# One order for the experts' stage on every engine, weights made in smaller steps, and first loads held back

## The chip, the cores and the metric

The kernel runs on one core of a Trainium2 chip. The core has five engines with a queue each: TensorE (PE; its weight loads are listed as PEld), VectorE (DVE), ScalarE (ACT), GpSimd (POOL) and SyncE (SP), which here issues all DMAs. An engine takes the instructions of its queue one after the other. The metric is the device time of one execution in microseconds; the median of several runs counts.

## What is computed

Attention with clusters, then a soft mixture of experts on its result. Sizes: 4 batches, 8 heads, 768 rows, 64 columns; 16 clusters; 8 experts with 512 x 1024 and 1024 x 512 weights, applied to all 3072 rows.

```python
q_assign = argmax(einsum('bhsd,hcd->bhsc', q_n, c_n))     # q_n, k_n, c_n: normalised rows
k_assign = argmax(einsum('bhsd,hcd->bhsc', k_n, c_n))
mask = q_assign[..., :, None] == k_assign[..., None, :]
attn = softmax(where(mask, scale * q @ k.T, -1e9))
x = (attn @ v) transposed to [3072, 512]
P = exp(x @ w_gate - max); 8 times: rows to sum 1, columns to sum 1, times N / E
out = sum over e of P[:, e:e+1] * (max(x @ w1[e], 0) @ w2[e])
```

## The kernel before

**Attention.** The class Planner (line 58) runs one generator ("process") for each piece of a head's work: load_pair (q and k of two heads), load_group (v of four heads, with their sums), split_part, assign_pair and place_pair (clusters, mask, and moves between tiles by DMA), max_chunk and max_rows (row maxima), exp_chunk, values, norm, out_batch (stores x of a batch to HBM as xd[b], and the gate logits lg), first_x (splits the first batch's x for the experts) and scan_first (largest weights of expert 0, 8 times two loads into a tile with one buffer, each followed by a reduce on VectorE). A process yields an engine with an assumed cost, or an event or token to wait for; the planner's own clock and the keys in KEYS decide who issues next. After every step keep_order ties each new instruction to the one before it on its engine, so the queues hold attention's work in just the planned order. The planner orders; it does not wait on the chip.

**Experts' stage.** x and w1 are split in 16-bit high and low parts, and layer 1 of two blocks of 128 hidden columns is one step of Winograd's form of Strassen's scheme: seven products instead of eight. The loop over order takes (batch, expert) in the order (0,0), (1,0), (0,1), (1,1), ... for batches 0 and 1, then the same for 2 and 3. Each has NP2 = 4 blocks f2, so there are 128 iterations t, four for each of 32 pairs. An iteration runs layer1: seven products m = 0 to 6 (product, L1173; six matmuls each), which are evicted by add (DVE, L1195) or scaled (ACT, L1200); relu_split makes hh (ACT, L1184) and the remainder hl (DVE, L1185). Between the products the loop calls step(before): layer2 of the iteration before, six blocks of rows of six matmuls (L1235 to L1237), accumulated in PSUM over the four f2 and, after the last, weighted by the gate into acc (done, L1253 and L1255). PSUM holds two tiles h_ps for the products and everything else small (ps_h, h_tile), and six for layer 2.

Beside this the loop steps through other generators, some pieces per iteration, by the number m of the product just issued:
- making: make_w makes one set of weights (wa, wb) of a pair of blocks from raw tiles r1, r2 (two buffers, wp0 and wp1): a scaling of r1 (ACT, L1083), four sums (GpSimd, L1093), casts on ScalarE with a remainder on GpSimd for three groups (L1096 and L1097; L1104 and L1105; for wb L1101 and L1102), and a scaling of r2 (L1099). begin(idx) says in which iteration set idx is started; load_raw loads the next set's raw tiles (L1070, L1074) then. For batch 0 each set is stored to HBM (store_w, L1110, L1111); the other batches load it from there (load_w, L1116, L1117). Made sets have three buffers.
- scanning: scan finds the largest weights of a later expert, eight loads of 512 KB in two tiles (L279, L283), each followed by a reduce (DVE, L286), and then the scale through two small matmuls (powers, L238 and L248); scan_at says in which iteration it starts.
- inputs: next_x loads the next batch's four parts xq (L1149), takes their largest (L286), makes four differences (less, L296) and splits seven parts into high and low (L300 on ACT, L303 on DVE).
- sink: gates, the exponential and eight rounds of normalisation of the gates (L1021 to L1048).

In this stage nothing calls keep_order. The framework's scheduler places each instruction by its own estimate of times, within the data dependencies, and so may move work of this stage in front of other work on an engine, into attention's end too. Tiles of pools opened after attention lie where attention's pools (nat first) lay, and wait for their last readers there.

## Time and profile before

| | us |
|---|---|
| median of 3 runs | 2497.99 (2495.38 to 2498.4) |
| profiled execution, its own time | 2494.76 |
| its span, first to last instruction | 2492.9 |
| TensorE busy with matmuls | 2386.4 (96%) |
| VectorE / ScalarE / GpSimd busy | 1374.5 / 834.8 / 651.5 |
| mean granted share of TensorE's clock | 0.987 |

Times in the rows are counted from the span's start. A matmul's end is modelled, so TensorE shown as busy need not be at its peak: the distance of starts tells more. In a timeline a row is start, duration, engine (with q where it is the queue's own instruction, such as a DMA issue), line, operation, output<-inputs, shapes and count; brackets hold the engine's idle time before it and what ended it. The granted clock has two levels, 1.2 and 2.4 GHz; a share between them is a mean over a stretch.

### The profile page before, as it was taken

Reading aid. Unit: us, or ns where it says so; the run is one execution under the profiler, and the core shown is the slowest. Engines: PE = TensorE matmul, PEld = TensorE weight load, DVE = VectorE, ACT = ScalarE, POOL = GpSimd, SP = SyncE. Lnnn points to the kernel's source line nnn. Section 1 sums busy time; section 2 is a strip of 40 time slices with the busy share of each in tenths; the row PEclk is TensorE's granted clock in tenths of the full one; section 3 lists DMA queues with packets and bytes.
Section 4 is the critical chain, followed back from the end, with each engine's and each line's share of the span. In section 5 each row is a group of like instructions: output and inputs, shape, how many; then the busy total and the mean of one; then the engine's idle time right before and its main releaser. Section 6 shows DMA issues by size and latency. Waiting matters only on the chain.

```text
span 2492.9 us, 32750 instructions
## 1 busy us (share of the span) xinstructions
PE 2386.4 (96%) x12848; PEld 1275.2 (51%) x12848; DVE 1374.5 (55%) x2385; ACT 834.8 (33%) x1610; POOL 651.5 (26%) x697
## 2 busy tenths in 40 slices
PE   6999999987898999999999999999999999999999
PEld 3655555543444455555454555555555555555554
DVE  7888888859674544444444446544443444444443
ACT  3555555554333333333424222222121222212221
POOL 4776767753323323241414100000000000000000
PEclk8999999988999999999999999999999999999999
DMA  7555454337766442434333314332222223222322
GB/s 162 134 118 131 97 123 91 104 146 270 271 238 229 155 154 101 158 113 141 132 124 133 123 43 144 104 112 95 93 103 106 94 93 109 101 93 94 114 103 89
DMA packets 154683, 320.30 MB, mean 128 GB/s; under 512 B 61088, under 2 KB 90528, under 8 KB 154016
## 3 DMA queue, kind: packets, MB, share of 16 engines
q1 hardware_dynamic: 154528, 318.21, 40.0%
q8 instruction: 101, 1.65, 0.3%
q14 instruction: 54, 0.44, 0.1%
HBM read 230.74 MB, written 58.72 MB: 116 GB/s over the span
## 4 chain that ended last, share of the span: by engine, by line
PE 72%; POOL 8%; DVE 8%; DMA 6%; issue 4%; ACT 2%; SPq 0%; POOLq 0%; ACTq 0%; DVEq 0%
PE h_ps L1173 28%; PE o_ps L1235 10%; PE o_ps L1236 10%; PE o_ps L1237 10%; PE av_ps L817 3%; POOL r L1093 3%; DMA r<-in_moe_w 3%; PE max_ps L690 2%; PE exp_ps L758 2%; DMA scan<-in_moe_w 2%; DVE mrt L694 2%; PE exp_ps L759 2%; POOL wa L1105 2%; POOL wb L1102 2%; POOL wa L1097 1%
## 5 line engine op out<-in xcount | busy, mean ns | idle before, releaser
L1173 PEld LDWEIGHTS <-wa 128*128 128x128 f16 x5376 | 529.0, 98 | 474.7 <-issue 54.3
L1185 DVE SCALAR_TENSOR_TENSOR hl<-c,hh 128x384 f16<-128x384 f32 x512 | 312.5, 611 | 544.5 <-ACT hh L1184 544.3
L1173 PE MATMUL h_ps<-xsT,wa 128*128 128x384 f16 x3072 | 588.7, 328 | 12.8 <-DVE u L1195 6.7
L1237 PE MATMUL o_ps<-wb,hl 128*128 128x512 f16 x1536 | 583.6, 380 | 4.9 <-DVE hl L1185 4.9
L1235 PE MATMUL o_ps<-wb,hh 128*128 128x512 f16 x1536 | 584.2, 380 | 0.0
L1236 PE MATMUL o_ps<-wb,hh 128*128 128x512 f16 x1536 | 584.1, 380 | 0.0
L1184 ACT ACTIVATE hh<-c 128x384 f16<-128x384 f32 x512 | 266.9, 522 | 854.2 <-DVE c L1195 850.4
L1173 PE MATMUL h_ps<-xsB,wa 128*128 128x384 f16 x2304 | 425.6, 329 | 19.8 <-DVE c L1195 18.8
L1237 PEld LDWEIGHTS <-hl 128*128 128x128 f16 x1536 | 150.7, 98 | 186.7 <-DVE hl L1185 7.4
L1195 DVE SCALAR_TENSOR_TENSOR c<-h_ps,u 128x384 f32<-128x384 f32 x256 | 142.0, 555 | 181.7 <-PE h_ps L1173 180.0
L784 POOL TENSOR_TENSOR psum<-psum,pe 128x512 f32<-128x512 f32 (+1 forms) x198 | 215.9, 1107 | 51.4 <-ACT pe L765 46.2
L1195 DVE SCALAR_TENSOR_TENSOR u<-h_ps,m 128x384 f32<-128x384 f32 x256 | 141.8, 554 | 157.1 <-PE h_ps L1173 156.8
L1235 PEld LDWEIGHTS <-hh 128*128 128x128 f16 x1536 | 150.8, 98 | 140.4 <-issue 1.8
L1236 PEld LDWEIGHTS <-hh 128*128 128x128 f16 x1536 | 150.8, 98 | 139.6 <-issue 1.3
L694 DVE TENSOR_REDUCE mrt<-max_ps 128x1 f32<-128x512 f32 (+1 forms) x288 | 190.6, 682 | 32.0 <-PE max_ps L690 29.7
L1200 ACT ACTIVATE c<-h_ps 128x384 f32<-128x384 f32 x128 | 62.5, 489 | 412.3 <-PE h_ps L1173 412.2
L765 ACT ACTIVATE pe<-exp_ps 128x512 f32<-128x512 f32 x288 | 166.4, 596 | 90.9 <-PE exp_ps L759 82.5
L1097 POOL TENSOR_TENSOR wa<-r,wa 128x256 f16<-128x256 f32 (+1 forms) x62 | 59.7, 982 | 389.0 <-ACT wa L1096 389.0
L1255 DVE SCALAR_TENSOR_TENSOR acc<-o_ps,gates,acc 128x512 f32<-128x512 f32 x168 | 125.3, 746 | 45.0 <-PE o_ps L1237 45.0
L817 PE MATMUL av_ps<-pe,vn 128*64 128x512 f32 (+1 forms) x768 | 134.4, 492 | 0.0
L690 PE MATMUL max_ps<-kX,qX 96*128 96x256 f32 (+1 forms) x384 | 125.7, 388 | 7.2 <-DVE mrt L694 6.3
L1093 POOL TENSOR_TENSOR r<-r 128x256 f32<-128x256 f32 x124 | 97.5, 807 | 122.9 <-ACT r L1083 114.7
(195 smaller groups left out, 1988.1 us busy)
## 6 DMA issues: line engine op xcount, KB each, us to landing
wa<-wd SPq DMA_DIRECT2D x96, 896.0 KB
wb<-wd SPq DMA_DIRECT2D x96, 512.0 KB
r<-in_moe_w SPq DMA_DIRECT2D x64, 512.0 KB
wd<-wa SPq DMA_DIRECT2D x32, 896.0 KB
scan<-in_moe_w SPq DMA_DIRECT2D x56, 512.0 KB
wd<-wb SPq DMA_DIRECT2D x32, 512.0 KB
qn<-in_q SPq DMA_DIRECT2D x16, 384.0 KB
kn<-in_k SPq DMA_DIRECT2D x16, 384.0 KB
```

Source lines behind the costliest of these rows:

```text
L690: nc.tensor.matmul(ps[:, y * (z - a) : (y + 1) * (z - a)], t["qa"][0:96, i * P : (i + 1) * P], t["k2"][0:96, a:z], start=True, stop=True)
L694: nc.vector.tensor_reduce(out=t["mr"][:, i0 : i0 + ni, ni - 1], in_=ps.rearrange("p (x c) -> p x c", x=ni), axis=AX, op=ALU.max)
L784: (nc.gpsimd if e == POOL else nc.vector).tensor_tensor(out=st[:, a:z], in0=old[a], in1=part, op=ALU.add)
L817: nc.tensor.matmul(av[o, a:z], vn[:, i, :], heads[t]["pe", c][:, i - i0], start=(i == 0), stop=False, skip_group_check=True)
L1093: by.tensor_tensor(out=S_[:, o], in0=a, in1=b_, op=op)
L1173: nc.tensor.matmul(ps[:, 0:HB], wa[:, w_, a, c, :], x[:, x_, c, :], start=(first and s_ == 0), stop=(s_ == len(steps) - 1), skip_group_che ...
L1184: nc.scalar.activation(hh[:, 2 - i, o], src, AF.Relu)
L1185: nc.vector.scalar_tensor_tensor(out=hl[:, 2 - i, o], in0=src, scalar=0.0, in1=hh[:, 2 - i, o], op0=ALU.max, op1=ALU.subtract)
L1195: nc.vector.scalar_tensor_tensor(out=t, in0=ps[:, 0:HB], scalar=KAPPA, in1=x, op0=ALU.mult, op1=ALU.add)
L1235: nc.tensor.matmul(po[i], hh[:, t, ti], wbh[:, t], start=(first and t == 0), stop=False)
L1236: nc.tensor.matmul(po[i], hh[:, t, ti], wbl[:, t], start=False, stop=False)
L1237: nc.tensor.matmul(po[i], hl[:, t, ti], wbh[:, t], start=False, stop=(last and t == 1))
```

## The change

- Experts' stage: keep_order is called after each product of layer 1 with all that is stepped beside it, and at the end. So every engine's queue keeps the order of the trace, behind attention's last instruction on that engine.
- The remainder hl is kept back in a list (rests) and issued after the steps of sink, scanning and inputs, before layer 2's block and the weights.
- The steps go to other m: sink at 0, 3, 5; scanning at 0 and 3 (in iterations 7 to 10 also 2 and 5); inputs at 0, 2, 3, 5, 6. Before it was odd m for sink, m = 1 and 4 for scanning (in the first four iterations 1, 3, 4, 5), even m for inputs.
- make_w has five steps instead of six, in the order: scaling and sums; scaling of r2; the first casts; the casts of the sums; wb.
- The sets of expert 1 start in iterations 7, 8, 9, 10 instead of 4, 6, 8, 10, its neighbour's scan (expert 2) in 7 instead of 4; both scans have an iteration by which they are run to their end (6 and 10).
- next_x has two empty steps after its loads; its differences are computed on GpSimd, the first two earlier.
- Attention: load_pair from the third pair on waits until the maxima of head 0 are placed (ev rows 0), load_group of the second group until those of head 1 are; scan_first waits before each of its eight rounds for the values of heads 16 to 23. The v tiles get a pool of their own (vals).

```diff
@@ -291,9 +291,9 @@
     LESS = {"T2": (("T1", "B12", "B11"), ("T2", "B22", "T1")), "B21": (("T4", "B21", "T2"), ("T3", "B22", "B12"))}
     xq, xs = {}, [{} for _ in range(B)]
-    def less(o, a, c):
+    def less(o, a, c, by=nc.vector):
         t = tmp.tile([P, KC, HB], F32, name="tx")
-        nc.vector.tensor_tensor(out=t, in0=xq[a], in1=xq[c], op=ALU.subtract)
+        by.tensor_tensor(out=t, in0=xq[a], in1=xq[c], op=ALU.subtract)
         xq[o] = t
     def split_hi(b, o):
@@ -310,6 +310,7 @@
         brief = actx.enter_context(tc.tile_pool(name="brief", bufs=1))
         work = actx.enter_context(tc.tile_pool(name="work", bufs=2))
         sm = actx.enter_context(tc.tile_pool(name="sm", bufs=2))
+        vals = actx.enter_context(tc.tile_pool(name="vals", bufs=2))
         ps_m = actx.enter_context(tc.tile_pool(name="ps_m", bufs=2, space=PSUM))
         ps_s = actx.enter_context(tc.tile_pool(name="ps_s", bufs=2, space=PSUM))
         ps_x = actx.enter_context(tc.tile_pool(name="ps_x", bufs=2, space=PSUM))
@@ -468,7 +469,7 @@
         def load_pair(p):
             b, hp_ = divmod(p, NP)
-            if p > 1 and GATES[0]:
+            if p > 1:
                 yield ev["rows", 0]
             yield t_nat
             t = pairs[p] = {}
@@ -483,9 +484,11 @@
             b, g = n // H, n % H // G
             hs = slice(g * G, (g + 1) * G)
             yield t_vn
+            if n == G:
+                yield ev["rows", 1]
             t = groups[(b, g)] = {}
             yield SP, 0.625
-            vn = nat.tile([P, G, NT, D], F32, name="vn", bufs=2)
+            vn = vals.tile([P, G, NT, D], F32, name="vn")
             nc.sync.dma_start(
                 out=vn.rearrange("p h t d -> p h (t d)"), in_=v[b, hs].rearrange("h (p t) d -> p h (t d)", t=NT)
             )
@@ -954,6 +957,7 @@
         def scan_first():
             am8 = sm.tile([P, 2, NF], F32, name="am8", bufs=1)
             for f in range(NF):
+                yield ev["v", nheads // 2 + f]
                 for m in range(2):
                     yield SP, 0.625
                     t = sm.tile([P, 512], F32, name="scan0", bufs=1)
@@ -1081,7 +1085,6 @@
         wa, wb = wt
         raw = r1[:, 0 : 4 * KC * P]
         nc.scalar.activation(raw, raw, AF.Copy, scale=s1[:, e : e + 1])
-        yield
         A = raw.rearrange("p (k c t f) -> p t k c f", k=2, c=KC, t=2)
         S_ = r1[:, 4 * KC * P :].rearrange("p (o c f) -> p o c f", o=4, c=KC)
         for o, a, b_, op in (
@@ -1092,17 +1095,17 @@
         ):
             by.tensor_tensor(out=S_[:, o], in0=a, in1=b_, op=op)
         yield
+        nc.scalar.activation(r2, r2, AF.Copy, scale=s2[:, e : e + 1])
+        yield
         for o, a in ((A22, A[:, 0, 1]), (slice(A11, A12 + 1), A[:, 1])):
             nc.scalar.copy(wa[:, 0, o], a)
             by.tensor_tensor(out=wa[:, 1, o], in0=a, in1=wa[:, 0, o], op=ALU.subtract)
         yield
-        nc.scalar.activation(r2, r2, AF.Copy, scale=s2[:, e : e + 1])
+        nc.scalar.copy(wa[:, 0, 3:7], S_)
+        by.tensor_tensor(out=wa[:, 1, 3:7], in0=S_, in1=wa[:, 0, 3:7], op=ALU.subtract)
         yield
         nc.scalar.copy(wb[:, 0], r2)
         by.tensor_tensor(out=wb[:, 1], in0=r2, in1=wb[:, 0], op=ALU.subtract)
-        yield
-        nc.scalar.copy(wa[:, 0, 3:7], S_)
-        by.tensor_tensor(out=wa[:, 1, 3:7], in0=S_, in1=wa[:, 0, 3:7], op=ALU.subtract)
         yield
     def store_w(idx, wt):
@@ -1147,16 +1150,21 @@
             k, j = divmod(i, 2)
             xq[o] = pers.tile([P, KC, HB], F32, name=f"xq{o}", tag=xq_from[o][1])
             nc.sync.dma_start(out=xq[o], in_=xd[b][:, k * KC : (k + 1) * KC, j * HB : (j + 1) * HB])
+        yield
+        yield
         for i, o in enumerate(XQ):
             largest(am4[:, i : i + 1], xq[o].rearrange("p c s -> p (c s)"))
             yield
+        for t, a, c in LESS["T2"]:
+            less(t, a, c, nc.gpsimd)
         am = gs.tile([P, 1], F32, name="am")
         nc.vector.tensor_reduce(out=am, in_=am4, axis=AX, op=ALU.max)
         for _ in input_scale(b, am, h_tile, gs):
             yield
         for o in XS:
-            for t, a, c in LESS.get(o, ()):
-                less(t, a, c)
+            if o == "B21":
+                for t, a, c in LESS[o]:
+                    less(t, a, c, nc.gpsimd)
             if b % 2:
                 xs[b][o] = xp.tile([P, 2, KC, HB], F16, name=f"xs{o}")
             else:
@@ -1179,12 +1187,18 @@
                 skip_group_check=not first,
             )
+    rests = []
+
     def relu_split(src, i, j, hh, hl):
         o = slice(j * HB, (j + 1) * HB)
         nc.scalar.activation(hh[:, 2 - i, o], src, AF.Relu)
-        nc.vector.scalar_tensor_tensor(
-            out=hl[:, 2 - i, o], in0=src, scalar=0.0, in1=hh[:, 2 - i, o], op0=ALU.max, op1=ALU.subtract
-        )
+
+        def rest():
+            nc.vector.scalar_tensor_tensor(
+                out=hl[:, 2 - i, o], in0=src, scalar=0.0, in1=hh[:, 2 - i, o], op0=ALU.max, op1=ALU.subtract
+            )
+
+        rests.append(rest)
     def layer1(wt, x, hh, hl):
         def c_tile(name):
@@ -1275,11 +1289,11 @@
     def begin(idx):
         e, j = divmod(idx, NP2)
-        return j - 1 if e == 0 else NP2 + 2 * j if e == 1 else 2 * NP2 * e + 2 * j - NP2 - 1
+        return j - 1 if e == 0 else 2 * NP2 + j - 1 if e == 1 else 2 * NP2 * e + 2 * j - NP2 - 1
     made = {}
     begins = {begin(i): i for i in range(NI)}
-    scan_at = {1: 0, 2: NP2, **{e: 2 * NP2 * (e - 1) - NP2 - 1 for e in range(3, E)}}
+    scan_at = {1: 0, 2: 2 * NP2 - 1, **{e: 2 * NP2 * (e - 1) - NP2 - 1 for e in range(3, E)}}
     sink, scanning, making, inputs = gates(), iter(()), iter(()), iter(())
     before = iter(())
     accs = {}
@@ -1314,25 +1328,26 @@
             if nb is not None:
                 nidx = ne * NP2 + (f2 + 1) % NP2
                 wn = load_w(nidx) if nb else None
-            early = t < NP2
             hh = hp.tile([P, 2, S], F16, name="hh")
             hl = hp.tile([P, 2, S], F16, name="hl")
             for m, _ in enumerate(layer1(wt, xs[b], hh, hl)):
+
+                if m in (0, 3, 5):
+                    step(sink)
+                if m in (0, 3) or m in (2, 5) and 7 <= t < 11:
+                    step(scanning)
+                if m in (0, 2, 3, 5, 6):
+                    step(inputs)
+                while rests:
+                    rests.pop(0)()
                 step(before)
                 step(making)
-                if m % 2 == 1:
-                    step(sink)
-                    if early or m == 1:
-                        step(scanning)
-                else:
-                    step(inputs)
-                    if m == 4:
-                        step(scanning)
+                plan.keep_order()
             for _ in before:
                 pass
             for x in (
                 (sink, inputs) if end else (),
-                (scanning,) if t == NP2 - 1 else (),
+                (scanning,) if t in (2 * NP2 - 2, 3 * NP2 - 2) else (),
                 (making,) if t + 1 in begins else (),
             ):
                 for y in x:
@@ -1344,6 +1359,7 @@
             t += 1
     for _ in before:
         pass
+    plan.keep_order()
 # ---- launch: one core; inputs and outputs as the reference has them ----
```

## Rows read from the trace of the kernel before

**Rows 1.** The page's second part: busy tenths of TensorE in forty slices
```profile
PE   6999999987898999999999999999999999999999
```
**Rows 2.** The chain of waits near the end: start, us, what
```profile
2450.51 1.95 PE h_ps L1173 x12
2465.11 1.95 PE h_ps L1173 x12
```
**Rows 3.** Windows: stretch, length, busy us (instructions) by engine, granted clock, DMA share
```profile
0.00:50.00 50.00, 28.73 (x95) 15.61 (x96) 36.25 (x97) 15.87 (x32) 21.36 (x36) 0.90 0.83 175
50.00:500.00 450.00, 427.79 (x2544) 258.80 (x2544) 382.29 (x625) 254.88 (x564) 326.60 (x395) 0.99 0.49 113
...
531.09:616.08 84.99, 65.64 (x321) 32.44 (x322) 66.51 (x155) 36.55 (x53) 28.23 (x26) 0.85 0.73 269
616.08:806.40 190.32, 170.40 (x862) 86.04 (x862) 121.73 (x178) 67.21 (x111) 66.59 (x59) 0.96 0.70 245
806.40:1486.20 679.80, 664.77 (x3528) 345.07 (x3526) 311.02 (x534) 230.15 (x394) 192.56 (x164) 1.00 0.37 127
1486.20:2492.90 1006.70, 1002.25 (x5352) 523.48 (x5350) 440.06 (x778) 214.02 (x423) 0.00 (x0) 1.00 0.29 103
```
**Rows 4.** Waits of ScalarE from 806.4 to 1486.2: us, times, longest
```profile
ACT r L1083 <- DMA r<-in_moe_w: 30.9, 10, 4.2
```
**Rows 5.** Timelines of ScalarE and of TensorE around 1230
```profile
1230.57 1.15 ACT L1083 ACTIVATE r<-r,s 128x1024 f32<-128x1024 f32 x1 [4.09 <-DMA r<-in_moe_w]
...
1233.45 1.14 PE L1173 MATMUL h_ps<-xsB,wa 128*128 128x384 f16 x6 [1.81 <-DVE c L1195]
```
**Rows 6.** Waits of VectorE from 616.08 to 806.4: us, times, longest
```profile
DVE am L286 <- DMA scan<-in_moe_w: 21.0, 16, 3.4
```
**Rows 7.** The chain of waits, one piece of the second stretch
```profile
658.23 9.53 DMA scan<-in_moe_w
```
**Rows 8.** Groups of VectorE from 531.09 to 616.08: count, busy us, mean ns, idle before
```profile
L286 DVE TENSOR_REDUCE am<-scan 128x1 f32<-128x1024 f32 x11 | 13.3, 1205 | 0.0
L1185 DVE SCALAR_TENSOR_TENSOR hl<-c,hh 128x384 f16<-128x384 f32 x13 | 7.9, 620 | 3.4 <-ACT hh L1184 3.4
```
**Rows 9.** Timeline of all engines at the seam, 498 to 537
```profile
498.36 0.94 DVE L286 TENSOR_REDUCE am<-xqB 128x1 f32<-128x768 f32 x1
...
524.75 0.38 SPq L1070 DMA_DIRECT2D r<-in_moe_w  x1
...
528.91 1.15 ACT L1083 ACTIVATE r<-r,s 128x1024 f32<-128x1024 f32 x1
...
531.09 1.14 PE L1173 MATMUL h_ps<-xsB,wa 128*128 128x384 f16 x3
...
531.93 0.34 SPq L915 DMA_DIRECT2D xd<-xT  x1
...
536.69 0.33 PE L944 MATMUL misc_ps<-ident,gt 96*128 96x96 f32 x2
```
**Rows 10.** Timelines of GpSimd and of VectorE around 577
```profile
576.44 2.46 POOL L1102 TENSOR_TENSOR wb<-r,wb 128x1024 f16<-128x1024 f32 x1 [0.34 <-ACT wb L1101]
...
576.84 2.10 DVE L1036 TENSOR_SCALAR rsum<-rsum 128x24 f32<-128x24 f32 x1
```
**Rows 11.** Timelines of SyncE, ScalarE, VectorE and TensorE, 11 to 35 us
```profile
11.18 0.51 SPq L281 DMA_DIRECT2D scan<-in_moe_w  x1
...
18.08 1.35 ACT L628 ACTIVATE ot<-misc_ps,om_bias,om_scale 64x384 f32<-64x384 bf16 x2 [1.08 <-PE misc_ps L621]
...
21.84 0.58 SPq L636 DMA_DIRECT2D qX<-ot  x1
...
28.96 0.68 DVE L286 TENSOR_REDUCE am<-scan 128x1 f32<-128x512 f32 x1
...
29.67 0.35 SPq L283 DMA_DIRECT2D scan<-in_moe_w  x1
...
34.12 1.20 PE L690 MATMUL max_ps<-kX,qX 96*128 96x512 f32 x2
```

## Prediction

> **What bounds the kernel now.** I read the page's strip of forty slices first [rows 1]: TensorE shows 9 from the fourteenth slice to the end, with lower digits in the first slice and in most of the ninth to thirteenth (500 to 810 us). Then the chain of waits, for the pace of an undisturbed iteration t of the experts' stage: the piece "x12" is the last product of one iteration and the first of the next, and two neighbours stand 14.60 us apart [rows 2]. Then windows cut at such pieces [rows 3]. An iteration is 42 + 36 = 78 matmuls, so their counts give 4 iterations from 531.09 to 616.08, 11 to 806.40, 45 to 1486.20 and 68 to the end. At 14.60 us these would take 58.4, 160.6, 657.0 and 992.8 us; they take 85.0, 190.3, 679.8 and 1006.7 (the last includes the final layer 2 and stores, about 14 us). TensorE is thus the bound of the last stretch, and 26.6 + 29.7 + 22.8 = 79 us of the three before are holes or half clock (granted share 0.85 and 0.96 in the first two). No change of order can win more there than these 79 us. The first 50 us hold only 28.7 us of matmuls [rows 3].
>
> **The change part by part. First, the holes of iterations 15 to 59 (22.8 us).** The waits show what ended ScalarE's idle time: the first scaling of a weight set stood 30.9 us in ten waits for its load, the longest 4.2 us [rows 4]. The timeline shows how that reaches TensorE: at 1230.57 ScalarE has sat 4.09 us before a scaling whose data had not come; the relu that the next sum needs stands behind it, VectorE behind that, and TensorE idles 1.81 us before the product at 1233.45 [rows 5]. ScalarE takes its work in a fixed queue, and in before nothing ties the making of weights to an iteration, so sets run in a burst, faster than the two raw buffers refill. With the order as traced, a set starts every second iteration and its raw load was issued an iteration pair (29 us) earlier; between the pieces of one set lie a product and a block of layer 2 (2.3 us). The sums of S (on GpSimd) are asked for three steps after they start, and wb, whose buffer comes free last, is now the last step. So nearly all of the hole goes; I leave 0.5 us for each of five experts, where ScalarE still waits for a wb buffer until layer 2 has read it. Gain 20.5 (ends 12 and 23).
>
> **Iterations 4 to 14 (29.7 us).** The same waits view for VectorE: the reduces of the scan wait for their load 16 times, 21.0 us together, 3.4 at the longest [rows 6]; a scan load lies 9.53 us in the chain at 658.23 [rows 7]. VectorE's queue holds the evictions of the products behind them. In before the scans are run far ahead: 11 reduces already in the first four iterations [rows 8], and the DMA engines are 70% busy in this stretch against 37% in the next [rows 3]. After, the scan of expert 1 takes two steps per iteration over t = 0 to 6, that of expert 2 four per iteration over t = 7 to 10, the later ones two. In t = 4 to 6 nothing but a scan stands beside the products. In t = 8 and 9 there are 1.4 MB of stores, 1 MB of raw load and 2 MB of scan, 4.4 MB per 14.6 us or 300 GB/s, against 269 GB/s moved at a share of 0.73 in the first stretch [rows 3], so some 370 were the engines full. That fits, barely: the scan load issued at the start of t = 8 or 9 lies behind 2.4 MB, some 8 to 9 us by that rate, and is asked for 6.8 us later. Two such waits of 2 us lie mostly under the two products for which an eviction may be late; I put 4 us on the path. Gain 25 (ends 15 and 29).
>
> **The seam and iterations 0 to 3.** Here the change costs. In before the scheduler put work of the experts' stage in front of attention's last steps: reduces of the next batch's input run at 498.36, the first raw load is issued at 524.75, before the last store of x at 531.93, and the first product runs at 531.09, before the last gate transposes at 536.69 [rows 9]. All of this goes back behind attention on its engine. The raw load then follows the store of x (1.5 MB) on SyncE's queue: issued about 532.5, it has those 1.5 MB in front of it (4.1 us at 370 GB/s, worked out above) and then its own 4.2 us, as in before (issued 524.75, used 528.91): about 540.8. Two scalings of 1.15 and the casts take some 3.3, so the first product starts about 544, 13 us later than now (TensorE's idle time to there brings the half clock for some us). The next batch's input loads stand on SyncE behind the stores of the first set, which wait for VectorE (about 547), and behind some 3.5 to 4 MB; the first reduce over them, though two steps later than before, waits until about 557, with VectorE's whole queue behind it. From then VectorE is the bound. It was busy 66.5 us of this stretch [rows 3]. Taken away: five of eleven scan reduces at 1.2 us [rows 8], 6.0, and two subtractions now on GpSimd, priced like a reduce over the same 768 columns at 0.94 [rows 9], 1.9. Added: three more reduces over the input that now run here, 2.8, and three relu remainders at 0.62 [rows 8] (16 belong to four iterations, 13 stand here) with an eviction, 2.4. That makes 64, and 66 with the 2 us of the next paragraph; begun at 541 and with some 9 us of waits for data and for TensorE in t = 0 and 1, it ends about 616, where iteration 4 starts today. I take +1 (ends -8, if the raw load lands as fast as now and the inputs come early, and +14, if VectorE's waits are not filled by anything).
>
> On GpSimd a subtraction of 768 columns lies between a quarter-size and the 1024-column one, so below 2.5 us [rows 10]; four per batch, about 7 us, beside three weight sets of 9 us each in 58 us: hidden. While GpSimd runs such an operation VectorE's small scalar operations can stand still: one took 2.10 us and ended with the 2.46 us operation of GpSimd that covers it [rows 10]. I allow 2 us for this within the stretch. The page GPSIMD Engine Reference of the Trainium skill, Key points, speaks against the move: it puts elementwise work about twice as fast on VectorE and says that the two share SBUF interfaces, with contention for VectorE instructions in a two-port mode or with two SBUF inputs. The pair of rows just named agrees. If that rule set the time, it would be the third rival below.
>
> **The start.** The values of the second group, the first scan load (11.18) and a third pair's q and k stand in front of the small moves. SyncE sends the first piece of the mask at 21.84 and then stands until 29.67, because the second scan load waits for a reduce that runs at 28.96; the other pieces of the mask come behind it. The first maxima run at 34.12, 4.4 us after SyncE moves on [rows 11]. The mask itself was made from 18.08 to 19.43. After, none of these loads is in front: the same 4.4 us from 19.4 give the first maxima at about 24, 10 us earlier, and a little more where the moves no longer share the DMA engines. The third pair now loads when head 0's maxima are placed, about 35; it is needed some two heads later, 30 us on, so that wait costs nothing. The scan of expert 0 moves to heads 16 to 23: 16 reduces, no more than now. Since TensorE is busy 428 of 450 us from 50 to 500 [rows 3], an earlier start carries through, less what a changed plan loses. Gain 9 (ends 0 and 13). The new pool for the values costs nothing by itself: the raw load that waited for the last heads now waits for its queue.
>
> **After 1486** both kernels run products and layer 2 in the same order; the late relu remainders have no other work in front of them. 0 (ends -1 and +3, for the inputs of batches 2 and 3, whose subtractions ScalarE may now await).
>
> **Sum.** -9 + 1 - 25 - 20.5 + 0 = -53.5. On the profiled execution's 2494.76 (span 2492.9) that is 2441.3; the median of the runs, 2497.99, lies 3.2 above it, so 2444; I say 2443. All ends together give 2421 and 2489.
>
> **The rivals.**
> One, the start's gain is lost: the planner's new order packs attention 9 us worse. For it: waits were added to a plan whose order all hangs together. Against: the cover of 30 us. 2452, chance 0.18.
> Two, the seam costs its upper end: raw load and inputs come late and VectorE idles, +13. For it: the queue of SyncE as told; the scan load of 11.18 was reduced only at 28.96 [rows 11]. 2456, chance 0.15. The page DMA: Bandwidth & Descriptors of the Trainium skill, Queues, rings and completion order, says that each DMA engine consumes its descriptors in ring order; by that rule a raw load behind the store of x gains nothing from being small, which is this rival's side.
> Three, GpSimd's subtractions block VectorE: four in the bound stretch, each holding a scalar operation for 2.1 us [rows 10], 8 us. 2451, chance 0.09.
> Four, slower than before: a fixed order makes every late load a stop. 56 scan reduces stand in VectorE's queue in front of evictions. If each waited 3.4 us, the longest of [rows 6], and 1 us of that were not covered, that is 56, and the gain of 53.5 is gone: 2500, and 2505 with the seam's cost. It decides when a scan load takes longer than two steps, 14.6 us for most and 6 to 8 us for t = 7 to 10; the longest in the chain is 9.53 [rows 7], which speaks against it for all but expert 2. Chance 0.09.
> Five, the change does not do what it says: the scheduler's order was already nearly that of the trace, or the holes come from elsewhere. [rows 9] speak against it. 2498, chance 0.04.
>
> **How the numbers follow.** The forecast has 0.45. It and rivals one to three (0.87 together) end faster by more than 0.2% (5 us, about what a measurement can tell from no change); five is the same, 0.04; four slower, 0.09. For 8 in 10 I leave out four and the tails of the forecast: 2416 to 2474.
>
> **What would show it.** Right: first maxima near 24 us; the first raw load issued after the last store of x; the piece x12 every 14.6 us from about t = 4 on; GpSimd busy in nine-us blocks every second iteration; no ScalarE wait for raw loads. Wrong: reduces of the scan with idle time before them in t = 15 to 59, holes at regular places, iteration 4 later than 620, or attention ending no earlier than 537.

## The result, and the profile after

The changed kernel takes 2471.32 us (median of six runs, 2468.96 to 2477.99), the kernel before 2498.19 beside it: a ratio of 0.9903, 95% interval 0.9889 to 0.9917, some 27 us less. The forecast was 2443; the time lies inside the range of 2416 to 2474 given with it, near its upper end, but the change is half of the one forecast. The profiled execution took 2472.1 us, its span 2470.3.

Windows of the changed kernel, columns as in [rows 3]. The cuts are the first product of iterations 0, 4, 15 and 60, about 1 us later than the chain's pieces in [rows 3]:
```profile
0.00:50.00 50.00, 35.89 (x123) 22.31 (x123) 36.67 (x96) 18.09 (x35) 23.64 (x40) 1.00 0.72 151
50.00:500.00 450.00, 434.39 (x2572) 259.15 (x2572) 382.50 (x628) 258.87 (x574) 334.98 (x403) 0.99 0.49 114
500.00:531.77 31.77, 20.42 (x126) 10.19 (x122) 11.46 (x20) 11.03 (x23) 9.36 (x11) 0.83 0.34 116
531.77:627.51 95.74, 64.76 (x298) 32.22 (x299) 67.96 (x137) 33.90 (x51) 35.91 (x28) 0.84 0.49 173
627.51:794.11 166.60, 162.49 (x867) 84.29 (x864) 89.75 (x154) 61.18 (x102) 53.92 (x48) 1.00 0.50 185
794.11:1462.78 668.67, 660.44 (x3527) 344.14 (x3526) 332.71 (x561) 238.20 (x402) 199.52 (x178) 1.00 0.44 160
1462.78:2470.30 1007.52, 1001.89 (x5347) 522.49 (x5345) 439.83 (x778) 213.54 (x423) 11.26 (x6) 1.00 0.28 103
```
The kernel before, cut in the same way, and the sum's terms beside what they came to (us; "attention" ends with the start of the last gate transposes on TensorE, the seam runs from there to the first product of iteration 4):

| | attention's end | seam | t = 4 to 14 | t = 15 to 59 | from t = 60 | span |
|---|---|---|---|---|---|---|
| before | 536.8 | 80.3 | 190.2 | 679.8 | 1005.9 | 2492.9 |
| after | 524.5 | 103.1 | 166.6 | 668.7 | 1007.5 | 2470.3 |
| measured | -12.3 | +22.8 | -23.6 | -11.1 | +1.6 | -22.6 |
| forecast | -9 | +1 | -25 | -20.5 | 0 | -53.5 |

Three terms hold within 3.5 us. The seam is 22 us dearer than said and the long stretch gains 9 less; those two make the miss.

### The profile page after: what moved, and what is told of

Read it like the earlier page. It is cut to its first block, busy times and chain, and to the rows that moved or that the text cites. A ratio compares the mean times of both kernels' runs of the same rounds, so it can differ in the third digit from the quotient of the medians.

```text
span 2470.3 us, 32700 instructions
## 1 busy us (share of the span) xinstructions
PE 2380.3 (96%) x12848; PEld 1274.8 (52%) x12848; DVE 1360.9 (55%) x2372; ACT 834.8 (34%) x1608; POOL 668.6 (27%) x712
## 4 chain that ended last, share of the span: by engine, by line
PE 87%; DVE 8%; ACT 2%; DMA 1%; issue 1%; POOL 1%; SPq 0%; ACTq 0%; DVEq 0%; POOLq 0%
PE h_ps L1181 34%; PE o_ps L1251 13%; PE o_ps L1249 13%; PE o_ps L1250 13%; PE av_ps L820 4%; PE max_ps L693 3%; PE exp_ps L761 2%; PE exp_ps L762 2%; DVE mrt L697 2%; DVE hl L1197 1%; PE misc_ps L553 1%; DVE vsum L503 1%; POOL psum L787 0%; DVE am L286 0%; ACT pe L768 0%
## 5 line engine op out<-in xcount | busy, mean ns | idle before, releaser
L787 POOL TENSOR_TENSOR psum<-psum,pe 128x512 f32<-128x512 f32 (+1 forms) x203 | 221.6, 1109 | 48.3 <-ACT pe L768 41.8
L1096 POOL TENSOR_TENSOR r<-r 128x256 f32<-128x256 f32 x124 | 88.7, 736 | 511.7 <-ACT r L1087 509.3
L762 PE MATMUL exp_ps<-qX,kX 98*128 98x512 f32 (+1 forms) x384 | 127.9, 346 | 0.0
```

The costliest lines, as they stand in the source:

```text
L762: nc.tensor.matmul(o, t["k2"][0:98, ki], t["qa"][0:98, a:z], start=False, stop=True)
L787: (nc.gpsimd if e == POOL else nc.vector).tensor_tensor(out=st[:, a:z], in0=old[a], in1=part, op=ALU.add)
```

## Where the time stands in the changed kernel

**The start and the first load.** Timelines of the changed kernel; a row is start, duration, engine, line, what, and in brackets the idle time before it and what ended it. Line 693 is the maxima's matmul, 918 the store of x, 1074 the raw load, 1087 the first scaling, 1181 the product:
```profile
23.75 1.19 PE L693 MATMUL max_ps<-kX,qX 96*128 96x512 f32 x2 [2.38 <-DMA qX<-ot]
```
```profile
520.42 0.34 SPq L918 DMA_DIRECT2D xd<-xT  x1
520.87 0.38 SPq L1074 DMA_DIRECT2D r<-in_moe_w  x1
...
524.31 0.39 PE L947 MATMUL misc_ps<-ident,gt 96*128 96x96 f32 x2 [0.56 <-DVE gt L941]
...
528.43 1.15 ACT L1087 ACTIVATE r<-r,s 128x1024 f32<-128x1024 f32 x1 [9.80 <-DMA r<-in_moe_w]
...
531.77 2.10 PE L1181 MATMUL h_ps<-xsB,wa 128*128 128x384 f16 x6 [7.07 <-ACT wa L1101]
```
The first maxima start at 23.75 (34.12 in [rows 11]); attention ends 12.3 us earlier (table). The raw load goes out behind the store of x and is used 7.56 us after its issue, against 4.16 in [rows 9]; TensorE stands 7 us and its next six matmuls take 2.10 us, twice what they take later (1.14 for six).

**The seam.** Waits of VectorE and of TensorE in the changed kernel, from 531 to 627.51 (us in total, times, longest). Line 286 is a reduce, 1209 an eviction, 1033 and 1047 are small matmuls of the gates, 240 the read of a small transpose:
```profile
DVE am L286 <- DMA xqB<-xd: 8.3, 1, 8.3
DVE hl L1197 <- ACT hh L1194: 4.4, 7, 1.2
DVE c L1209 <- PE h_ps L1181: 4.3, 2, 2.2
DVE xsT L303 <- ACT xsT L300: 3.5, 2, 2.0
```
```profile
PE h_ps L1047 <- DVE c L1209: 10.1, 4, 5.4
PE h_ps L1033 <- DVE c L1209: 9.2, 1, 9.2
PE h_ps L1181 <- ACT wa L1101: 7.1, 1, 7.1
PE h_ps L1181 <- DVE gm L240: 4.8, 1, 4.8
```
TensorE waits for VectorE and VectorE, a little later, for TensorE and ScalarE. A point where one engine can go on only with what another has just finished is called a hand-over below. Two places of the timeline show how. First the inputs' load, asked for when it has not come:
```profile
539.51 2.34 SPq L1152 DMA_DIRECT2D xqB<-xd  x4
...
547.13 0.95 DVE L286 TENSOR_REDUCE am<-xqB 128x1 f32<-128x768 f32 x1 [8.28 <-DMA xqB<-xd]
548.00 0.55 DVE L1209 SCALAR_TENSOR_TENSOR c<-h_ps,u 128x384 f32<-128x384 f32 x1
...
549.61 0.55 DVE L1209 SCALAR_TENSOR_TENSOR c<-h_ps,m 128x384 f32<-128x384 f32 x1
...
550.22 0.58 PE L1033 MATMUL h_ps<-g,ones 1*128 1x1 f32 x2 [9.20 <-DVE c L1209]
```
The evictions behind that reduce in VectorE's queue come 8 us late, and a matmul of the gates, in front of the next products in TensorE's queue, waits 9.2 us for the PSUM tile that they free. Second, no load at all:
```profile
552.64 0.36 DVE L1042 TENSOR_TENSOR pr<-pr,rsum 128x192 f32<-128x192 f32 x1
...
564.06 0.27 PE L238 MATMUL h_ps<-ident,am 128*1 128x128 f32 x1 [0.60 <-DVE csum L1049]
...
566.17 2.11 POOL L1105 TENSOR_TENSOR wa<-r,wa 128x1024 f16<-128x1024 f32 x1
566.61 1.89 DVE L1042 TENSOR_TENSOR pr<-pr,rsum 128x192 f32<-128x192 f32 x1
568.53 0.49 DVE L1044 TENSOR_REDUCE csum<-pr 128x8 f32<-128x192 f32 x1
568.95 1.21 DVE L286 TENSOR_REDUCE am<-scan 128x1 f32<-128x1024 f32 x1
570.07 0.27 DVE L240 TENSOR_REDUCE gm<-h_ps 1x1 f32<-1x128 f32 x1
570.39 2.08 PE L1181 MATMUL h_ps<-xsT,wa 128*128 128x384 f16 x6 [4.77 <-DVE gm L240]
```
The product needs the tile that a small transpose (564.06) holds. VectorE could read it at once, but work of the gates and a scan reduce stand in front, and one operation of the gates takes 1.89 us beside a remainder that GpSimd makes for a weight set, where the same operation took 0.36 us at 552.64. TensorE waits 4.77 us, and runs at half clock behind it.

**Iterations 15 to 59.** ScalarE's waits from 793.3 to 1462, and the timeline at one of the six places:
```profile
ACT wb L1107 <- PE o_ps L1251: 14.7, 6, 2.5
```
```profile
835.22 0.56 DVE L1197 SCALAR_TENSOR_TENSOR hl<-c,hh 128x384 f16<-128x384 f32 x1 [0.59 <-ACT hh L1194]
...
837.64 1.04 ACT L1107 CAST wb<-r 128x1024 f16<-128x1024 f32 x1 [2.45 <-PE o_ps L1251]
...
838.59 0.52 ACT L1194 ACTIVATE hh<-c 128x384 f16<-128x384 f32 x1
838.76 2.12 POOL L1108 TENSOR_TENSOR wb<-r,wb 128x1024 f16<-128x1024 f32 x1 [4.22 <-ACT wb L1107]
839.14 2.15 DVE L1197 SCALAR_TENSOR_TENSOR hl<-c,hh 128x384 f16<-128x384 f32 x1 [2.24 <-ACT hh L1194]
...
839.61 0.38 PE L1250 MATMUL o_ps<-wb,hh 128*128 128x512 f16 x1
...
841.36 0.39 PE L1251 MATMUL o_ps<-wb,hl 128*128 128x512 f16 x1 [1.37 <-DVE hl L1197]
```
No ScalarE wait for a raw load is left (30.9 us in [rows 4]). A new one stands in its place: the copy into wb waits 2.45 us for layer 2 of the expert's first set, and the relu behind it is late. The relu's remainder on VectorE now falls beside GpSimd's remainder of wb, which starts when the late copy is done: it takes 2.15 us, where the same operation took 0.56 at 835.22, and TensorE waits 1.37 us for it. At 0.56 us it would have ended at 839.70; TensorE would have asked for it at about 839.82, some 0.2 us behind the start of the matmul before (839.61). So the late relu alone would have cost TensorE nothing there (an estimate from these rows; no run moves GpSimd's operation alone). At all six places the remainder takes 2.15 to 2.16 us, and the iteration 16.14 us, 1.54 more than an undisturbed one: 9.2 in six.

## The experiments

Each was timed beside the kernel before, whose median was 2497.1 to 2498.9. The theory to start with: the order kept in iterations 0 to 3 makes the seam's loss, and the copy into wb that of the long stretch. Rivals: late loads, GpSimd's subtractions, the work itself.

**Which part gains what.** start_only is the kernel before with attention's part alone (the waits of load_pair, load_group and scan_first, the pool vals). order_free leaves all calls of keep_order out of the experts' stage. order_from4 keeps them from iteration 4:
```diff
-                plan.keep_order()
+                if t >= NP2:
+                    plan.keep_order()
+                else:
+                    plan.skip_order()
...
+    def skip_order(self):
+        for i in self.instructions()[self.traced :]:
+            self.last[i.engine] = i.name
+        self.traced = len(self.instructions())
```


> The kernel before, with only attention's part of the change: the third pair's and the second values' loads wait for the first heads, the values have a pool of their own, the scan of expert 0 waits for the later heads. Theory, the start's 12 us (last gate transposes at 524.3 instead of 536.7) reach the end: 2498 - 12 = 2486. Rival, the free order of before had drawn the experts' work in front of attention's end, bound by other things, so that the start's gain is partly lost at the seam: 2490 to 2495.

Measured: 2478.65, ratio 0.9921 (0.9904 to 0.9937). More than was expected: 20 us, and 17 between the profiled spans (attention's end 15.4 earlier, at 521.4; the seam still 80.6; iterations 4 to 14 in 188.4). The rival falls: the start's gain goes right through.

> The changed kernel, but the order of the trace is kept in the experts' stage only from iteration 4 on; iterations 0 to 3 are left to the scheduler, as in before. Theory, the fixed order costs the seam its 22 us (from attention's last transposes to iteration 4 it took 102.4 us, 80.4 in before): the seam goes back to about 80, iteration 4 starts near 605 instead of 626.5, time 2471 - 22 = 2449. Rival, the seam is longer because of the work that the change moved there (three more reduces of the inputs, relu remainders, subtractions on GpSimd): the order doesn't matter, time 2468 to 2471.

Measured: 2439.55, ratio 0.9760 (0.9744 to 0.9777): 32 us below the changed kernel. The seam takes 73.2, less than in before; the stretches behind are those of the changed kernel (166.5, 668.7, 1007.5). The work moved there isn't the loss; its order is, with its place behind attention (the two are told apart below).

> The changed kernel with no order kept anywhere in the experts' stage; all its other edits stay (the steps of a weight set, the later scan and weight sets of experts 1 and 2, the remainders of the relus one step later, subtractions on GpSimd, attention's part). Theory: from iteration 4 on it is the kept order that gains (23.5 us in iterations 4 to 14, 11 in 15 to 59), so without it these come back: 2439.6 (order kept from iteration 4 on) + 35 = 2475. Rival: the other edits gain it and the order none: 2440.

Measured: 2464.65, ratio 0.9865 (0.9849 to 0.9882), between both. Seam 72.4, then 184.8, 669.7 and 1011.0. Waits of VectorE of this kernel in iterations 4 to 14, where the changed kernel has one wait of 4.2 us on such a load:
```profile
DVE am L286 <- DMA scan<-in_moe_w: 17.8, 14, 2.8
```
So, as this kernel stands, the kept order is worth 18.2 us in iterations 4 to 14, 1.0 in 15 to 59 and 3.5 later. In the long stretch the 1.0 is a balance. With the order free (order_free, 782.3 to 1452) ScalarE still waits for raw loads:
```profile
ACT r L1098 <- DMA r<-in_moe_w: 49.9, 14, 4.4
ACT r L1087 <- DMA r<-in_moe_w: 21.5, 13, 2.3
```
With it kept there is no such wait, but the six places of wb. Against these 23 us stand 30.7 us of the seam: kept everywhere, the order makes this kernel slower (2471.3 against 2464.7).

**The copy into wb.** wb_late, and from4_wb, which is order_from4 with the same edit:
```diff
+        if idx % NP2 == NP2 - 1:
+            yield
+            yield
         nc.scalar.copy(wb[:, 0], r2)
```


> The changed kernel with one edit: the last step of a weight set (the copy into wb) comes two steps later, in the last product of its iteration, for the last of an expert's four sets. Theory: ScalarE's wait for the wb buffer (2.45 us, once per expert, 14.7 us in six) goes, and with it the 2.05 us that each expert's three iterations take beyond 14.60; there are seven such places, so 2471 - 14 = 2457, at the least 12 off. Rival, the hole has another cause (the wait is covered, or the copy's later place makes the next thing late): under 4 us off, 2467 or more.

Measured: 2460.31, ratio 0.9844 (0.9829 to 0.9859), 11 us off. Iterations 15 to 59 take 659.4 instead of 668.7, and ScalarE no longer waits for layer 2. So the late copy is the cause of the six places, but the size is 9.3 there and 11 in all, where the theory allowed no less than 12. No remainder takes over 1.3 us in that stretch any more; but the run moves the copy and GpSimd's operation behind it together, so it doesn't part the late relu from the drawn-out remainder. The stretch is now 20.4 us shorter than in the kernel before.

> Both gains together: the order is kept from iteration 4 on only, and the copy into wb comes two steps later for an expert's last set. If the two losses are of different stretches, as the theory says, they add: 2439.6 - 11 = 2428.6. Rival, they share something (the later copy delays what the free order had hidden): 2434 or more.

Measured: 2429.60, ratio 0.9735 (0.9719 to 0.9751). The two add. This is the fastest version here, 42 us below the changed kernel.

**Place or order within.** two_chains forgets the chain's ends before the first raw load is traced; free_behind ties every instruction of iterations 0 to 3 to attention's last one on its engine and to nothing else:
```diff
+    plan.last, plan.traced = {}, len(plan.instructions())
     load_raw(0)
```


> The changed kernel, with the order of the trace kept inside attention and kept inside the experts' stage, but the experts' stage no longer tied behind attention's last instructions: it may run in between them. (With the order left free in iterations 0 to 3 the first product started at 515.7 instead of 531.8, and from there to iteration 4 it took 81.7 us instead of 95.7.) Theory: two separate losses, 16 for standing behind attention's end and 14 for the order within. This kernel gets the first back alone: first product near 516, 95 us from there to iteration 4, time 2471 - 16 = 2455. Rival one, the place is all (the long iterations come from loads that all start late): 2441. Rival two, the order within is all (an early first product waits the longer for the rest): 2468 to 2471.

> The other half of the same question: iterations 0 to 3 are left to the scheduler among themselves, but each of their instructions stays behind the last instruction of attention on its engine; from iteration 4 on the order is kept. Theory of two losses: first product near 531, 82 us from there to iteration 4, time 2471 - 14 = 2457. Rival one, the place is all: 2468 to 2471. Rival two, the order within is all: 2441.

Measured: two_chains 2463.07 (ratio 0.9871, 0.9853 to 0.9888), free_behind 2454.51 (0.9831, 0.9814 to 0.9847). The place alone is worth 8, the order within alone 17, both 32. In two_chains the first product starts at 511.6, 9.7 us before attention's end, but iteration 4 comes 105.9 us later: 10 of the 17 us by which it starts earlier (it stood 7.3 behind) are lost again. So there are two losses, but not as sized: the order within is the larger, and the place pays in full only when the order is free.

**Loads and GpSimd.** early_x issues the second batch's input loads behind the first two raw loads; two_early is that with two_chains; less_vec takes the subtractions back to VectorE:
```diff
+    inputs = next_x(1)
+    next(inputs)
     wt = made[0] = w_tiles(True)
...
```


> The changed kernel with one edit: the loads of the second batch's inputs are issued right behind the first two raw loads, before the first weight set is made, instead of behind the stores of the first set and the third raw load. Theory (TensorE and VectorE wait for each other in turn all through the seam, the late input is one stop among many): the 8.3 us wait of VectorE before the first input reduce goes, but only 3 to 5 us come off, 2466 to 2468. Rival, the late inputs are the seam's loss: 8 us or more come off, 2463 or less.

Measured: 2464.34, ratio 0.9860 (0.9845 to 0.9875): 7.0 off, between both expectations. The late inputs are a part of the seam's 22 us, not all of them.

> The order of the trace kept within attention and within the experts' stage, the stage free to run in between attention's last instructions, and the loads of the second batch's inputs issued right behind the first two raw loads. Alone the two edits gave 8.2 and 7.0 us on 2471.3. Rival: they add, 2456. Theory: with an early first product it is VectorE's wait for the late inputs (still 7.2 us there) that holds back the gain, so together they give some 7 us more: 2449.

Measured: 2459.68, ratio 0.9845 (0.9830 to 0.9860). Both expectations miss: only 3.4 us more than two_chains. The inputs' wait isn't what held the early start back.

> The changed kernel with the four subtractions of a batch's inputs back on VectorE. Rival (the prediction's third: GpSimd's subtractions block VectorE's small operations in the seam, about 2 us each): 2463 or less. Theory (they cost VectorE no more than they save it): 2468 to 2475.

Measured: 2471.56, ratio 0.9899 (0.9884 to 0.9913): no difference. On balance the subtractions on GpSimd neither cost nor save. The weight sets' operations run on GpSimd in this kernel too, so it doesn't test those.

**The small steps.** small_last traces the relu remainders and layer 2's block ahead of the gates', scan's and inputs' steps; fixed_best is that with two_chains, early_x and wb_late:
```diff
+                while rests:
+                    rests.pop(0)()
+                step(before)
                 if m in (0, 3, 5):
                     step(sink)
...
-                while rests:
-                    rests.pop(0)()
-                step(before)
                 step(making)
```


> The changed kernel with one edit: in each step of an iteration the block of layer 2 and the relu remainder are traced ahead of the gates', the scan's and the inputs' small steps, not behind them. The small matmuls borrow the second PSUM tile of the products, so they wait for VectorE's eviction, and the next product waits until VectorE has read them. Theory (these hand-overs are the order's loss in iterations 0 to 3): the block of layer 2 covers them, 6 us off (4 to 10), 2465. Rival (VectorE's work of 67 us binds there, whatever the order): 2469 to 2472.

Measured: 2485.43, ratio 0.9949 (0.9934 to 0.9963): 14 us slower, 5 of it in the seam, 7 in iterations 15 to 59. The theory's remedy was the wrong way round. A small matmul that borrows a tile waits twice, for the eviction before it and, through the next product, for VectorE's read after it; layer 2's block had covered the second. The timeline of small_last shows that wait, which the changed kernel doesn't have there, at five places 120 us apart; two iterations at each take 15.78 and 15.31 us instead of 14.70 and 15.01, which makes the 7 us. The 5 us of the seam were not followed to their places.
```profile
821.06 0.27 PE L238 MATMUL h_ps<-ident,am 128*2 128x128 f32 x1
821.27 0.75 DVE L1269 SCALAR_TENSOR_TENSOR acc<-o_ps,gates,acc 128x512 f32<-128x512 f32 x1 [0.74 <-PE o_ps L1251]
821.93 0.27 DVE L240 TENSOR_REDUCE gm<-h_ps 2x1 f32<-2x128 f32 x1
822.25 1.14 PE L1181 MATMUL h_ps<-xsT,wa 128*128 128x384 f16 x6 [0.92 <-DVE gm L240]
```


> All four edits at once, with the order of the trace kept throughout the experts' stage: free to run in between attention's last instructions, early input loads, layer 2's block ahead of the small steps, the late copy into wb. Theory: an order fixed in advance loses nothing against a free one if hand-overs are covered and loads are early: within 8 us of the 2429.6 of the free seam, 2430 to 2437. Rival: a fixed order in the seam costs something that these three edits don't reach: 2440 or more.

Measured: 2461.50, ratio 0.9852 (0.9837 to 0.9867). It carries the loss of small_last, so it doesn't tell what the best fixed order would give; that stays open.

**Which queue.** As free_behind, but one engine alone is free in iterations 0 to 3 and the others keep the order of the trace.

> The changed kernel, but in iterations 0 to 3 VectorE's order is left to the scheduler (behind attention's last instruction); every other queue keeps the order of the trace. All queues free in this way gave 2454.5, none 2471.3. Theory: VectorE's queue is the one that costs (its scan and input reduces, the gates' and the third weight set's work stand in front of the evictions and reads for which TensorE waits): 10 us or more off, 2461 or less. Rival: the loss is in another queue, or only in several together: 2466 or more.

> The same with TensorE's order alone left free in iterations 0 to 3. Rival theory: the small matmuls of the gates and the inputs stand in TensorE's queue in front of products and blocks of layer 2 that could run: 10 us or more off, 2461 or less. If VectorE's queue is the cause: under 5 off, 2466 or more.

> The same with ScalarE's order alone left free in iterations 0 to 3. Rival theory: the scalings and casts of the weight sets stand in ScalarE's queue in front of the relus and scalings of sums: 10 us or more off, 2461 or less. If VectorE's queue is the cause: under 5 off, 2466 or more.

> The same with SyncE's order of DMA issues alone left free in iterations 0 to 3. Early loads of the inputs alone had given 7.0 us. Rival theory (late loads): 7 us or more off, 2464 or less. If it is VectorE's queue: 0 to 6 off, 2465 to 2471.

| free in t = 0 to 3 | time | ratio (95%) | below 2471.3 | seam |
|---|---|---|---|---|
| VectorE | 2458.46 | 0.9841 (0.9824 to 0.9858) | 12.9 | 90.2 |
| TensorE | 2465.84 | 0.9878 (0.9855 to 0.9902) | 5.5 | 98.5 |
| ScalarE | 2468.82 | 0.9885 (0.9863 to 0.9907) | 2.5 | 98.9 |
| SyncE | 2469.81 | 0.9886 (0.9868 to 0.9904) | 1.5 | 99.3 |
| all (free_behind) | 2454.51 | 0.9831 (0.9814 to 0.9847) | 16.8 | 86.8 |

VectorE's queue holds most of it: freed alone, it gives 13 of the 17 us. The singles sum to 22 us against 17 for all together, so they overlap. TensorE's 5.5 is just over the 5 that the theory left it; the last two are no larger than the spread of their runs. The window of vec_free from its first product to iteration 4, and its timeline of VectorE where the inputs are reduced (its lines stand 14 further on):
```profile
528.10:611.13 83.03, 62.14 (x298) 31.38 (x299) 67.31 (x136) 33.71 (x51) 36.64 (x28) 0.89 0.57 213
```
```profile
544.09 1.21 DVE L300 TENSOR_REDUCE am<-scan 128x1 f32<-128x1024 f32 x1
545.22 0.15 DVE L1063 TENSOR_SCALAR csum<-h_ps 128x8 f32<-128x8 f32 x1
545.29 1.21 DVE L300 TENSOR_REDUCE am<-scan 128x1 f32<-128x1024 f32 x1
546.42 0.94 DVE L300 TENSOR_REDUCE am<-xqB 128x1 f32<-128x768 f32 x1
```
The work is the same (67.3 us), the idle time 15.7 us instead of 27.8. The first input reduce runs at 546.42 without idle time before it: VectorE has done evictions and gates' work in the time in which it stood for 8.28 us in the changed kernel.

## Why the prediction was wrong

**The seam is the step that failed.** Its events were right: the raw load behind the store of x, a first product 13 us later than in before against attention's own end, VectorE's work (66 us said, 67.96 measured). The mis-sized term is "some 9 us of waits for data and for TensorE": VectorE is idle 95.74 - 67.96 = 27.8 us, 19 more, nearly all of the 22. The first wait for inputs, 8.28 us, alone fills the 9; the rest is the hand-over in both directions, which the sum had as a share of VectorE's own time and not as a chain through two queues. It is the order that makes it, VectorE's above all: free_behind and vec_free change nothing else, and 17 and 13 us come back. The sign that the prediction named for this, iteration 4 later than 620, is there (627.51). Rival two had the side right and the price, 13, too low; it named late loads, and early_x gives only 7. The Trainium skill's rule of ring order (DMA: Bandwidth & Descriptors, Queues, rings and completion order) stood on that side too; the first load agrees with it, used 7.56 us after its issue behind the store of x and 4.16 in front of it.

The prediction also took as settled that everything goes back behind attention. It costs 8 to 15 us by the runs (two_chains; order_from4 against free_behind) and isn't a part of what gains: the order from iteration 4 on gives the same with a free seam.

**Iterations 15 to 59**: 20.5 said, 11.1 measured, just outside the lower end of 12. The remainder was put at 0.5 us for each of five experts. That much is there without any wait: in both kernels two iterations per expert take 14.70 and 15.01 us, those with a scan's small matmuls. What the sum left out are the six places of wb, 1.54 us each, 9.2 together. Their start was named, ScalarE waiting for a wb buffer until layer 2 has read it, but not what hangs on it: the relu queued behind, and the remainder that then runs beside GpSimd's operation. That the kept order ends the waits for raw loads is right, and with the late copy (wb_late) the stretch gains 20.4. The gain of 11 that the changed kernel shows here is there without the order too (order_free, 669.7); what a late copy would give with a free order was not run.

**Iterations 4 to 14** came as said, 23.6 for 25. The one late scan load stands in the timeline at iteration 8:
```profile
699.13 1.22 DVE L286 TENSOR_REDUCE am<-scan 128x1 f32<-128x1024 f32 x1 [4.17 <-DMA scan<-in_moe_w]
```
Two waits of 2 us were allowed for it; TensorE lost 1.33 and 1.13 us there, waiting for evictions behind it.

**The start** gave 12.3 for 9, within its ends (10 to 18 by the profiles of kernels with the same attention, below); attention's part alone, start_only, gave 20 between the medians, above the upper end of 13; the first maxima stood at 23.75 for "about 24". Rival one falls. **After 1486**: +1.6, within its ends. One sum was off: on the profiled execution's 2494.76 the upper ends together make 2485, not 2489.

**GpSimd** (rival three). Single operations stand still as told: the 128x192 product of the gates takes 1.89 us beside GpSimd's 2.11 us operation (566.61, above) and 0.36 at 552.64. What the Trainium skill says of contention (GPSIMD Engine Reference, Key points) shows in that row. The rival's price for the subtractions moved to GpSimd doesn't show: less_vec gives 2471.56. The weight sets' operations, which run on GpSimd in both kernels, do have a price in the changed one, that of the six places of wb; the prediction has no term for them. **Rival four** falls too: of the scan's reduces from iteration 4 to 14 one waits, not all.

## What to carry to other kernels

Price a fixed order stretch by stretch. Where loads and buffers leave slack it keeps bursts from forming (here 23 us after iteration 4); where three engines hand small pieces to each other, every late piece stops all that stands behind it, and the loss is in idle time, which a sum of busy times doesn't show: leave the order free there. Of a wait that is left over, price what is queued behind it on its engine, see what that then runs beside on other engines, and count its places.

## What the runs showed of the hardware

The same attention code ended between 518.9 and 526.7 us in the profiled executions of these kernels (wb_late and sca_free), 7.8 us apart; a difference of a few us between two profiles' starts is no finding. And the granted clock follows the stalls of the seam: mean 0.84 in the changed kernel, 0.89 in vec_free and 0.90 in order_from4 (from 515.65 to 597.31), so a stall costs more than its own length; six matmuls of a product took 2.08 us behind the wait of 4.77 us, and 1.14 us undisturbed.

In these rows VectorE's relu remainder and an operation of GpSimd take turns. From iteration 15 to 59 of the changed kernel 22 remainders began while GpSimd made the remainder of a wb (2.12 to 2.13 us), and each ended 0.41 to 0.42 us after it: 16 took 1.25 us and had begun 1.29 us into it, the six at the places of wb took 2.15 to 2.16 us and had begun 0.38 us into it. Where the remainder began first, 0.34 us ahead of a GpSimd operation (830.26, for one), it took 0.56 us.
